# Attention beside a fused expert layer: scores one tile ahead, the product with v cut at block boundaries, the sums of v earlier, and tasks that come at 0.8 and 0.7

## The chip, the cores and the metric

The kernel runs on one core of one Trainium2 chip. The metric is the time of one execution in microseconds (us) of device time; a time given for a kernel is the median of several executions. A profile shows one execution, with its own time.

## What is computed

There are three stages, all in float32. The first is attention over 8 batches, 8 heads, 576 queries and 64 channels, in which keys and values are first averaged over groups of 8 rows, so that each query meets 72 keys:

```python
k_p = k.reshape(B, H, Sp, pool, D).mean(axis=3)
v_p = v.reshape(B, H, Sp, pool, D).mean(axis=3)
scores = scale * np.matmul(q, k_p.transpose(0, 1, 3, 2))
scores = scores - np.max(scores, axis=-1, keepdims=True)
attn = np.exp(scores)
attn = attn / (np.sum(attn, axis=-1, keepdims=True) + 1e-09)
return np.matmul(attn, v_p).astype(np.float32)
```

Its output, as 4608 tokens of 512 channels, goes through `((x @ w1) * (x @ w2)) @ w3 @ w_out` and that through `relu(x @ w_in)**2 @ w_out2`. The wide products are made of three float32r products each (high and low parts of both operands).

## The kernel before

The kernel is laid out around TensorE (PE). A first stretch (`fold`) multiplies `w3 @ w_out` into one matrix W. Then come nine **blocks** of 512 tokens. A block has eight **units**: in a unit `stage_ab` runs 24 matmuls of x with w1 and w2 (`ps_w`, 512 columns each), VectorE (DVE) and ScalarE (ACT) multiply the two results and split them into `gt`, and two units later `stage_w` runs 12 matmuls with W (`acc`). After the ninth block the third stage fills the rest of the span; the change does not touch its code.

Attention is no stage of its own. `build_tasks` writes its work out as a list of small **tasks**, and `attend` takes tasks from that list at each tick. A tick comes after every 6 matmuls of a block. Each tick adds `rate[0]` to a credit; once the credit reaches `visit[0]`, tasks run while a credit of 1 is left. A task may name what must be done first (`need`); if that is missing the list stops there and the credit is capped at 3. At the start of a block `until(tokens_ready(...))` ticks on with no matmul of a block between, until all tokens of the block are there.

A batch has five tiles of queries (128 rows, the last 64), in two halves: tiles 0 and 1 (256 queries), and tiles 2 to 4 (320). For a tile g the tasks are: `pe_s` (two halves: scores `ps_s`, then maxima `mx` on DVE, eight exponentials into `att` on ACT, and on GpSimd, called POOL here, the division by the sums), `place_rem` (POOL copies the keys past the 128th into `rem`), and `pe_t` (part 0 transposes `att` into `ps_t`, part 1 transposes `rem`; ACT and DVE split the results into `aT` and `aR`). At the end of a half `pe_av` runs once for each of the four pairs of heads: four matmuls into `ps_av` with `vl` and `vr` (the pooled v, split), then ACT copies the high part and DVE subtracts the low part into the block's operand `x` (chunk `x_blk_c` of block blk). A half that lies across a block boundary needs the later block's buffers, so its tasks wait until the block two before that is through (`("ab", last - 2)`).

All of `ps_s`, `ps_t`, `ps_av` and `ps_kt` (the turned keys) share two PSUM buffers, the pool `ps_at`. A task whose buffer is not free yet holds up PE, which runs its instructions in order; ACT and DVE too run theirs in the order written.

v of a batch is loaded in five pieces and summed on DVE (`vp` four times, and `ends`, L325), then `cut` and `cut_odd` split the sums into `vl` and `vr`. There is one buffer of each. k goes the same way through `kp` and `ends` (L329), and both share one queue, `back["kv"]`, of which one part is done per tick. From the second block on, the same ticks also feed the **quarters**: pieces of w_in and w_out2 that are prepared on ACT and DVE (`rq`, `raw`, `wq`, `sq`, `oq`) for the third stage.

Of the kernel before, what the change touches and what calls it, by code (L numbers as in the profile page):

```python
# [16 lines left out]
TB = 512  # L17
# [18 lines left out]
def attn_moe_moe2_kernel(  # L36
# [17 lines left out]
    B, H, S, D = q.shape  # L54
# [6 lines left out]
    NP = H // 2  # L61
# [8 lines left out]
    QT = []  # L70
    s0 = 0
# [3 lines left out]
    HALF = [[0, 1], [2, 3, 4]]  # L75
# [24 lines left out]
    done = set()  # L100
# [256 lines left out]
    def load_v(b):  # L357


        def parted(hi, lo, src, row):  # L360

            nc.scalar.activation(hi, src, ACTF.Copy, scale=row)
            nc.vector.scalar_tensor_tensor(
                lo, src, row, f32(hi), op0=ALU.mult, op1=ALU.subtract)

        def cut():
            for x in range(2):
                parted(vl[:, 0, :, x, :], vl[:, 1, :, x, :], vp, rows[:, x:x + 1])

        def cut_odd():  # L370
            vo = vr.rearrange("p (a b) t d -> p b a t d", a=2)[:, :, :, 1]
            for x in range(2):
                row = rows[:RB, 2 + x:3 + x]
                parted(vo[:RB, x], vo[2 * RB:, x], v5, row)
                nc.scalar.activation(vo[RB:2 * RB, x], v5, ACTF.Copy, scale=row)
            done.add(("v", b))

        return kv_parts(v, b, lambda j: vp[:, j, :], [cut, cut_odd])

    def pe_kt(b, part):  # L380

# [75 lines left out]
    def pe_s(g, half):  # L457
        b, i = divmod(g, len(QT))
        s0, n = QT[i]
        hf = 0 if i in HALF[0] else 1  # L460
        c0 = s0 - QT[HALF[hf][0]][0]
        flush("q", (b, hf))
        t = qts[b, hf]
        ps = ps_at.tile([P, TB], F32, tag="at", name="ps_s")
        hs = NP // 2
        for x in range(hs):
            hp = half * hs + x
            nc.tensor.matmul(  # L468
                ps[:n, x * 2 * SP:(x + 1) * 2 * SP], t[:, hp, c0:c0 + n],
                kbd[:, hp].rearrange("p a s -> p (a s)"), start=True, stop=True)  # L470
        sv = ps[:n, :NP * SP].rearrange("p (h s) -> p h s", s=SP)
        a = att[g % 3]
        h0 = half * NP
        av = a[:n, :H * SP].rearrange("p (h s) -> p h s", s=SP)
        mx = at_p.tile([P, NP], F32, tag="mx", name="mx", bufs=2)
        if half == 0:
            sums[g] = at_p.tile([P, H], F32, tag="sm", name="sm", bufs=2)
        sm = sums[g]

        scale = 1.0 / (POOL * D ** 0.5)  # L480

        nc.vector.reduce_max(mx[:n], sv, axis=AX.X)
        nc.vector.tensor_scalar(mx[:n], mx[:n], -scale, None, op0=ALU.mult)  # L483
        for h in range(NP):
            nc.scalar.activation(  # L485
                av[:, h0 + h], sv[:, h], ACTF.Exp, bias=mx[:n, h:h + 1], scale=scale,
                accum_out=sm[:n, h0 + h:h0 + h + 1])
        if half == 0:
            return

        nc.vector.tensor_scalar(sm[:n], sm[:n], 1e-9, float(POOL), op0=ALU.add, op1=ALU.mult)
        nc.vector.reciprocal(sm[:n], sm[:n])
        nc.gpsimd.tensor_mul(av, av, sm[:n].unsqueeze(2).to_broadcast([n, H, SP]))

        if g < 2 * len(QT) + 1:
            place_rem(g)

    def place_rem(g):
        n = QT[g % len(QT)][1]
        a = att[g % 3]  # L500
        rems[g] = at_p.tile([P, 2, RR], F32, tag="rem", name="rem")
        for x in range(2):
            nc.gpsimd.tensor_copy(
                rems[g][:n, x].rearrange("p (i c s) -> p i c s", i=3, c=2),
                a[:n, x * 4 * SP:(x + 1) * 4 * SP].rearrange("p (c w) -> p c w", c=2)[:, :, P:]
                .unsqueeze(1).to_broadcast([n, 3, 2, RM]))

    def pe_t(g, part):
# [18 lines left out]
        nc.scalar.copy(rem[:, :, c0:c0 + n], ps[:RR, :2, :n])  # L527
        dl = rem[RB:2 * RB, :, c0:c0 + n]
        nc.vector.tensor_sub(dl, ps[RB:2 * RB, :2, :n], f32(dl))
        if 2 * len(QT) <= g < NG - 1:  # L530
            place_rem(g + 1)

    def pe_av(b, hf, hp):
        hi, lo, rem = atts[b, hf]
        s0 = QT[HALF[hf][0]][0]
        w = sum(QT[i][1] for i in HALF[hf])
        ps = ps_at.tile([P, TB], F32, tag="at", name="ps_av")
        st = [vl[:, i, hp].rearrange("p a d -> p (a d)") for i in range(2)]
        for m in mm3(ps[:, :w], [(st, [t[:, hp, :w] for t in (hi, lo)])], last=False):
            m()  # L540
        nc.tensor.matmul(
            ps[:, :w], vr[:, hp].rearrange("p a d -> p (a d)"), rem[:, hp // 2, :w],
            start=False, stop=True)
        t0 = b * S + s0
        pieces = []
        o = 0
        while o < w:
            blk, c = divmod(t0 + o, TB)
            n = min(w - o, TB - c)
            pieces.append((blk, c, o, n))  # L550
            o += n

        for blk, c, o, n in pieces:
            nc.scalar.copy(xt_tile(blk, hp)[:, 0, c:c + n], ps[:, o:o + n])
        for blk, c, o, n in pieces:
            t = xt_tile(blk, hp)
            nc.vector.tensor_sub(t[:, 1, c:c + n], ps[:, o:o + n], f32(t[:, 0, c:c + n]))  # L557
        done.add(("av", b, hf, hp))

    NG = B * len(QT)  # L560

    def s_end(hf):
        return QT[HALF[hf][-1]][0] + QT[HALF[hf][-1]][1]

    def build_tasks(first_k, first_v):
# [49 lines left out]
        for g in range(NG):  # L615
            b, i = divmod(g, len(QT))
            hf = 0 if i in HALF[0] else 1

            if g < 2 * len(QT):
                if g + 1 != len(QT):  # L620
                    ahead_of(g)
            else:
                if g == 2 * len(QT):
                    ahead_of(g)
                if g + 1 < NG:
                    ahead_of(g + 1)
            if i == HALF[hf][0]:
                put_pend(len(pend))
            for part in range(2):
# [3 lines left out]
                for fn in first_v:  # L633
                    put(fn)
            if i == HALF[hf][-1]:
                need = [("v", b)]

                last = (b * S + s_end(hf) - 1) // TB
                if last >= 2:
                    need.append(("ab", last - 2))  # L640
                for hp in range(NP):
                    def av(b=b, hf=hf, hp=hp):
                        pe_av(b, hf, hp)
                        if hf == 1 and hp == NP - 1 and b + 1 < B:
                            load_v(b + 1)
                    pend.append((need, av))
                if b < EARLY:
                    put_pend(len(pend))
            if g + 1 == len(QT):
# [23 lines left out]

    def tokens_ready(n):

        b, s = divmod(n, S)
        halves = [(bb, h) for bb in range(b) for h in range(2)]
        if s:
            halves.append((b, 0))
            if s > QT[HALF[1][0]][0]:  # L680
                halves.append((b, 1))
        return all(("av", bb, h, hp) in done for bb, h in halves for hp in range(NP))


    wt = {}
# [646 lines left out]
    hold_v[0] = False  # L1332
    pumps.append(feed_w12)
    until(lambda: tokens_ready(TB))
    rate[0] = 0.7
    visit[0] = 2.0

    late = []
# [35 lines left out]
    for i in range(NB):  # L1374
# [18 lines left out]
            pend.append((i, u))  # L1393
        done.add(("ab", i))
        if i == 1:
            rate[0] = 0.6
        if i == 0:
            until(lambda: not fh1)
            sec_p.release()
# [105 lines left out]
```

## Time and profile before

| | us |
|---|---|
| median of 3 runs | 1530.74 (1528.7 to 1532.65) |
| the profiled execution, its own time | 1529.85 |
| its span, first to last instruction | 1528.0 |
| PE busy in the span | 1492.2 |
| DVE busy | 1000.3 |
| ACT busy | 798.4 |

The span is 1.85 us shorter than the execution's own time, and that execution was 0.89 us below the median. PE is the engine that is busy nearly throughout.

### The profile page before, as it was taken

The numbers are of one execution on the slowest core, as the hardware profiler recorded it, in microseconds if no ns is written. First come the engines' busy times: TensorE is split into PE (matmuls) and PEld (weight loads), VectorE is DVE, ScalarE is ACT, GpSimd is POOL, SyncE is SP. The second block draws the span as 40 slices with busy tenths as digits, with TensorE's granted clock in tenths as the row PEclk, the third lists the DMA queues.
The fourth block names the chain that finished last, engine by engine and source line by source line (L and its number), as shares of the span: only waits on it lengthen the run. The fifth ranks groups of instructions, "written<-read, shape, count | busy, mean of one in ns | idle before, by whom it ended". The sixth has DMA issues, their size and how long they took to land.

```text
span 1528.0 us, 21290 instructions
## 1 busy us (share of the span) xinstructions
PE 1492.2 (98%) x6752; PEld 1200.6 (79%) x6752; DVE 1000.3 (65%) x1798; ACT 798.4 (52%) x1953; POOL 81.2 (5%) x144
## 2 busy tenths in 40 slices
PE   6899999999999999999999999999999999999998
PEld 3457778877888888878888888888888888888887
DVE  7988686676767477658245477759675967576542
ACT  6866465454545355545235575456445744464431
POOL 1011110101010011100000000000000000000000
PEclk9999999999999999999999999999999999999999
DMA  9545666566666657557539777777777777788752
GB/s 288 197 139 138 165 196 161 168 178 174 187 199 174 193 127 242 149 169 227 173 113 307 222 195 247 208 209 229 235 207 208 232 207 207 208 268 282 209 163 89
DMA packets 292783, 301.34 MB, mean 197 GB/s; under 512 B 119360, under 2 KB 184896, under 8 KB 292672
## 3 DMA queue, kind: packets, MB, share of 16 engines
q1 hardware_dynamic: 287488, 290.54, 65.3%
q10 hardware_dynamic: 5184, 9.44, 1.8%
q8 instruction: 55, 0.90, 0.2%
q14 instruction: 56, 0.46, 0.1%
HBM read 243.27 MB, written 56.62 MB: 196 GB/s over the span
## 4 chain that ended last, share of the span: by engine, by line
PE 71%; DVE 4%; ACT 2%; DMA 1%; issue 1%; ACTq 0%; DVEq 0%
PE o L1219 18%; PE ps_w L193 17%; PE acc L193 9%; PE ps_c L1117 5%; PE ps_a L1117 5%; PE ps_d L1117 5%; PE ps_h L193 3%; PE o L193 3%; PE ps_b L1117 3%; PE ps_s L468 1%; PE ps_av L193 1%; PE ps_t L521 1%; DVE gt L121 1%; DMA rq<-in_moe_w_in_dram 0%; ACT x2o L120 0%
## 5 line engine op out<-in xcount | busy, mean ns | idle before, releaser
L1219 PE MATMUL o<-gt,un 128*128 128x512 f32 x1344 | 329.4, 390 | 0.4
L1219 PEld LDWEIGHTS o<-gt,un 128*128 128x128 f32 x1344 | 251.9, 188 | 54.6 <-DVE gt L121 2.1
L121 DVE TENSOR_TENSOR gt<-gs,gt 128x512 fp32r<-128x512 f32 x240 | 164.9, 689 | 179.8 <-ACT gt L120 178.4
L193 PE MATMUL ps_w<-x,wt 128*128 128x512 f32 x960 | 240.7, 397 | 1.9 <-DVE x L557 0.9
L120 ACT CAST gt<-gs 128x512 fp32r<-128x512 f32 x240 | 148.5, 620 | 154.8 <-PE o L1219 88.0
L193 PE MATMUL acc<-gt,Wt 128*128 128x512 f32 x864 | 219.6, 397 | 0.0
L193 PEld LDWEIGHTS ps_w<-x,wt 128*128 128x128 f32 x960 | 175.5, 188 | 41.2 <-DVE x L557 2.7
L193 PEld LDWEIGHTS acc<-gt,Wt 128*128 128x128 f32 x864 | 160.6, 189 | 32.8 <-issue 0.8
L193 PE MATMUL ps_w<-x,un 128*128 128x512 f32 x768 | 184.5, 392 | 0.0
L193 PEld LDWEIGHTS ps_w<-x,un 128*128 128x128 f32 x768 | 142.5, 188 | 29.1 <-issue 0.2
L485 ACT ACTIVATE att<-ps_s,mx 128x72 f32<-128x72 f32 (+1 forms) x320 | 97.9, 323 | 49.0 <-DVE mx L483 48.6
L1124 ACT ACTIVATE r<-r 128x512 f32<-128x512 f32 x96 | 60.7, 632 | 118.8 <-DVE r L1154 118.3
L844 DVE TENSOR_TENSOR gf<-asb,ps_w 128x512 f32<-128x512 f32 x72 | 49.3, 685 | 75.1 <-PE ps_w L193 68.8
L1117 PE MATMUL ps_a<-x2o,un 128*128 128x512 f32 x384 | 97.5, 389 | 0.0
L1117 PE MATMUL ps_d<-x2o,un 128*128 128x512 f32 x384 | 97.5, 389 | 0.0
L1117 PE MATMUL ps_c<-x2o,un 128*128 128x512 f32 x384 | 97.5, 389 | 0.0
L1125 ACT ACTIVATE gs<-r 128x512 f32<-128x512 f32 x144 | 89.9, 629 | 3.6 <-DMA x2r<-x2d 2.0
L120 ACT CAST gt<-gf 128x512 fp32r<-128x512 f32 x72 | 44.8, 622 | 82.5 <-DVE gf L844 82.2
L1193 DVE TENSOR_TENSOR gs<-gs 128x512 f32<-128x512 f32 x128 | 86.5, 684 | 0.0
L1117 PEld LDWEIGHTS ps_d<-x2o,un 128*128 128x128 f32 x384 | 72.1, 188 | 15.0
L1117 PEld LDWEIGHTS ps_a<-x2o,un 128*128 128x128 f32 x384 | 72.1, 188 | 14.9
L1117 PEld LDWEIGHTS ps_c<-x2o,un 128*128 128x128 f32 x384 | 72.1, 188 | 14.9
(114 smaller groups left out, 1975.2 us busy)
## 6 DMA issues: line engine op xcount, KB each, us to landing
un<-u_w SPq DMA_DIRECT2D x128, 256.0 KB, 3.4
un<-u_A SPq DMA_DIRECT2D x128, 256.0 KB, 3.0
un<-u_S SPq DMA_DIRECT2D x128, 256.0 KB, 3.0
un<-u_oS SPq DMA_DIRECT2D x128, 256.0 KB, 3.0
un<-u_oA SPq DMA_DIRECT2D x96, 256.0 KB, 3.0
raw<-in_moe_w_dram SPq DMA_DIRECT2D x32, 512.0 KB, 5.3
raw<-in_moe_w_out_dram SPq DMA_DIRECT2D x24, 512.0 KB, 4.6
kv<-in_k_dram SPq DMA_DIRECT2D x32, 256.0 KB, 3.3
```

The lines of the kernel that those rows point to most:

```text
L120: nc.scalar.copy(hi, src)
L121: return (eng or nc.vector).tensor_sub(lo, src, f32(hi))
L193: (lambda a=a, b=b, i=i: nc.tensor.matmul(ps, a, b, start=first and i == 0, stop=last and i == n - 1))
L468: nc.tensor.matmul(ps[:n, x * 2 * SP:(x + 1) * 2 * SP], t[:, hp, c0:c0 + n], kbd[:, hp].rearrange("p a s -> p (a s)"), start=True, stop=True)
L485: nc.scalar.activation(av[:, h0 + h], sv[:, h], ACTF.Exp, bias=mx[:n, h:h + 1], scale=scale, accum_out=sm[:n, h0 + h:h0 + h + 1])
L521: nc.tensor.transpose(ps[:, c, :n], att[g % 3][:n, c * 2 * SP:c * 2 * SP + P], ident[:n, :n])
L844: front["dve"] = nc.vector.tensor_mul(gf, asb, pss[1])
L1117: nc.tensor.matmul(ps, l, r, start=first and j == 0, stop=j == len(todo) - 1, skip_group_check=True)
L1124: nc.scalar.activation(t, src, ACTF.Relu)
L1125: nc.scalar.activation(take(name), t, ACTF.Square)
L1193: d = nc.vector.tensor_sub(src, a, src)
L1219: nc.tensor.matmul(ob[x][o], l, r, start=u == 0 and m != 5 and j == 0, stop=u == NU - 1 and j == 2, skip_group_check=True)
```

## The change

Four things change. (1) Scores run one tile ahead of the transposes throughout (before, from the third batch on, two tiles ahead), with three `att` buffers as before; the copy into `rem` is again made right behind the scores, and `place_rem` is gone. (2) A half that lies across a block boundary is multiplied with v in two pieces, cut at the boundary: six of the sixteen halves, with pieces of 192 and 128, 128 and 192, 64 and 256, 192 and 64, 128 and 128, and 64 and 192 columns. Each piece has a need of its own, and a task then does two pairs of heads. (3) The sums of v of the next batch are queued once v of this batch is split (before: after the last product with it); the split itself follows the last product, or the sums if these come later. (4) The pace is 0.8 a tick instead of 0.7 from the first block, and 0.7 instead of 0.6 from the third.

```diff
             done.add(("v", b))
-
-        return kv_parts(v, b, lambda j: vp[:, j, :], [cut, cut_odd])
+            if b + 1 < B:
+                load_v(b + 1)
+
+        def summed():
+            done.add(("vs", b))
+            if b in cut_now:
+                cut()
+                cut_odd()
+
+        cuts_v[b] = [cut, cut_odd]
+        return kv_parts(
+            v, b, lambda j: vp[:, j, :], [cut, cut_odd] if b == 0 else [summed])
+
+    cuts_v = {}
+    cut_now = set()
+
+    def read_v(b):
+
+        if b + 1 == B:
+            return
+        cut_now.add(b + 1)
+        if ("vs", b + 1) in done:
+            for fn in cuts_v[b + 1]:
+                fn()
...
-        if 2 * len(QT) <= g < NG - 1:
-            place_rem(g + 1)
-
-    def pe_av(b, hf, hp):
+
+    def av_pieces(b, hf):
+
+        t0 = b * S + QT[HALF[hf][0]][0]
+        w = HWS[hf]
+        cut = TB - t0 % TB
+        if cut >= w or (t0 + cut) // TB < 2:
+            return [(0, w)]
+        return [(0, cut), (cut, w - cut)]
+
+    def pe_av(b, hf, hp, q0, w):
...
-            if g < 2 * len(QT):
-                if g + 1 != len(QT):
-                    ahead_of(g)
-            else:
-                if g == 2 * len(QT):
-                    ahead_of(g)
-                if g + 1 < NG:
-                    ahead_of(g + 1)
+            if g + 1 != len(QT):
+                ahead_of(g)
...
+                pieces = av_pieces(b, hf)
+                for q0, w in pieces:
+                    need = [("v", b)]
+                    last = (b * S + s_end(hf) - HWS[hf] + q0 + w - 1) // TB
+                    if last >= 2:
+                        need.append(("ab", last - 2))
+                    for hp in range(0, NP, len(pieces)):
+                        def av(b=b, hf=hf, hp=hp, q0=q0, w=w, n=len(pieces)):
+                            for x in range(hp, hp + n):
+                                pe_av(b, hf, x, q0, w)
+                            if hf == 1 and hp + n == NP and q0 + w == HWS[hf]:
+                                read_v(b)
+                        pend.append((need, av))
...
-    rate[0] = 0.7
+    rate[0] = 0.8
...
-            rate[0] = 0.6
+            rate[0] = 0.7
```

What this does to the order of instructions shows at the start of the third block (block 2). On PE, before, behind 12 matmuls with W (`acc`) of the last block, the products of batch 2's second half (320 columns, all four pairs of heads) stand apart, with other matmuls between them:

```order
L193 MATMUL ps_av_2845<-aT0_2415,vl_101 128x320
L193 MATMUL ps_av_2845<-aT1_2416,vl_101 128x320
L193 MATMUL ps_av_2845<-aT0_2415,vl_101 128x320
L541 MATMUL ps_av_2845<-aR_2417,vr_102 128x320
L193 MATMUL acc0_2254<-gt_2712,Wt_995 128x512 x2
L468 MATMUL ps_s_2855<-kbd_103,qT1_2476 128x144 x2
L193 MATMUL ps_w1_2907<-x_2_0_1896,wt_431 128x512 x3
```

On PE with the change, behind 12 matmuls with W and 6 of x with w1, the second piece of that half (192 columns) stands there with all four pairs of heads in one run. These are its last row of the second pair, the third and the fourth pair, and what follows:

```order
L563 MATMUL ps_av_2884<-aR_2371,vr_102 128x192
L193 MATMUL ps_av_2892<-aT0_2369,vl_101 128x192
L193 MATMUL ps_av_2892<-aT1_2370,vl_101 128x192
L193 MATMUL ps_av_2892<-aT0_2369,vl_101 128x192
L563 MATMUL ps_av_2892<-aR_2371,vr_102 128x192
L193 MATMUL ps_av_2900<-aT0_2369,vl_101 128x192
L193 MATMUL ps_av_2900<-aT1_2370,vl_101 128x192
L193 MATMUL ps_av_2900<-aT0_2369,vl_101 128x192
L563 MATMUL ps_av_2900<-aR_2371,vr_102 128x192
L537 MATMUL ps_t_2921<-ident_96,att0_104 128x128 x4
L193 MATMUL ps_w1_2868<-x_2_2_1984,wt_769 128x512 x3
```

The first piece (128 columns) has moved ahead into the block before, and 16 matmuls of the second, with a transpose behind them, stand in one piece. The same shape, four pairs in a run, stands at the starts of blocks 1, 6 and 7; at those of blocks 3 and 5 there are two runs of two pairs, with 4 matmuls and 1 matmul between.

On DVE at the same place, before, behind the product `gf` of the last unit, one sum of k is left, and the first low part of `x` is sixth:

```order
L329 TENSOR_REDUCE ends_98<-kv_2745 64x64
L482 TENSOR_REDUCE mx_2803<-ps_s_2800 128x4
L121 TENSOR_TENSOR gt_2816<-gf_2815,gt_2816 128x512
L483 TENSOR_SCALAR mx_2803<-mx_2803 128x4
L446 STREAM_TRANSPOSE qT0_2755<-qraw_2763 128x256
L557 TENSOR_TENSOR x_2_0_1896<-ps_av_2845,x_2_0_1896 128x128
L557 TENSOR_TENSOR x_3_0_2851<-ps_av_2845,x_3_0_2851 128x192
```

On DVE with the change, behind the same `gf`, four sums of k stand ahead of the first `x`, and the split of v for the next batch follows inside the run:

```order
L329 TENSOR_REDUCE kp_97<-kv_2585 128x64
L950 TENSOR_TENSOR oq_3116<-sq_3018,oq_3116 128x512
L121 TENSOR_TENSOR gt_2843<-gf_2842,gt_2843 128x512
L329 TENSOR_REDUCE kp_97<-kv_2836 128x64
L329 TENSOR_REDUCE kp_97<-kv_2854 128x64
L329 TENSOR_REDUCE ends_98<-kv_2863 64x64
L579 TENSOR_TENSOR x_3_0_2881<-ps_av_2876,x_3_0_2881 128x192
L579 TENSOR_TENSOR x_3_1_2889<-ps_av_2884,x_3_1_2889 128x192
L950 TENSOR_TENSOR oq_3177<-sq_3018,oq_3177 128x512
L579 TENSOR_TENSOR x_3_2_2897<-ps_av_2892,x_3_2_2897 128x192
L363 SCALAR_TENSOR_TENSOR vr_102<-ends_98,rows_100,vr_102 32x2x64
L363 SCALAR_TENSOR_TENSOR vl_101<-vp_99,rows_100,vl_101 128x4x64 x2
```

Four sums of k instead of one now stand between `gf` and the first `x`. At the start of block 1 four sums of k stand there too, two of them ahead of each of two groups of `x`.

On DVE in unit 3 of block 2, before, the last sum of v and the split of batch 3 stand directly ahead of the `x` of the first products with it:

```order
L325 TENSOR_REDUCE ends_98<-kv_3165 32x128
L482 TENSOR_REDUCE mx_3221<-ps_s_3218 64x4
L914 TENSOR_TENSOR sq_3299<-sq_3299,wq_3068 128x256
L363 SCALAR_TENSOR_TENSOR vr_102<-ends_98,rows_100,vr_102 32x2x64
L483 TENSOR_SCALAR mx_3221<-mx_3221 64x4
L844 TENSOR_TENSOR gf_3253<-asb_3196,ps_w2_3198 128x512
```

With the change these sums of batch 3 stand in units 2 to 4 of block 1, and its split at the start of block 2, as the rows above show.

## Rows read from the trace of the kernel before

**Rows 1.** Windows: length, busy us of each engine, granted clock, DMA share, GB/s.
```profile
120.00:710.00 590.00, 580.08 (x2801) 472.47 (x2800) 399.58 (x821) 309.60 (x1020) 66.25 (x114) 0.99 0.62 177
140.00:175.00 35.00, 32.25 (x150) 24.53 (x148) 30.82 (x61) 21.10 (x76) 6.10 (x9) 0.95 0.71 194
315.00:335.00 20.00, 17.82 (x83) 14.36 (x83) 15.60 (x31) 10.23 (x27) 1.99 (x3) 0.91 0.56 160
710.00:1528.00 818.00, 813.02 (x3583) 671.61 (x3582) 500.37 (x777) 402.28 (x691) 0.00 (x0) 1.00 0.71 211
```

**Rows 2.** Waits of PE from 120 to 710 us: total us, times, longest.
```profile
PE ps_av L541 <- DVE vr L363: 2.2, 1, 2.2
PE ps_t L521 <- issue: 2.0, 1, 2.0
PE ps_s L468 <- ACT att L485: 1.1, 2, 0.9
PE ps_av L193 <- DVE vl L363: 0.9, 2, 0.6
PE ps_w L193 <- DVE x L557: 0.9, 2, 0.5
PE ps_av L193 <- ACT vl L362: 0.6, 1, 0.6
PE ps_av L193 <- DVE x L557: 0.5, 2, 0.3
```

**Rows 3.** Timeline, 317 to 321 us: start, us, engine, instruction [idle before <-releaser].
```profile
317.21 1.09 PE L193 MATMUL acc<-gt,Wt 128*128 128x512 f32 x4
...
320.49 0.36 PE L541 MATMUL ps_av<-aR,vr 96*128 96x256 f32 x1 [2.18 <-DVE vr L363]
```

**Rows 4.** Timeline, 145 to 148 us: maxima of two halves, then a transpose.
```profile
145.40 0.24 DVE L483 TENSOR_SCALAR mx<-mx 128x4 f32<-128x4 f32 x2
...
147.08 1.02 PE L521 MATMUL ps_t<-ident,att 128*128 128x128 f32 x4 [2.03 <-issue]
```

**Rows 5.** Timeline of PE: spacing of matmuls of 256, 512 and 64 columns.
```profile
237.90 0.51 PE L193 MATMUL ps_av<-aT,vl 128*128 128x256 f32 x3
...
238.85 1.55 PE L193 MATMUL acc<-gt,Wt 128*128 128x512 f32 x6
240.24 2.89 PE L193 MATMUL ps_w<-x,un 128*128 128x512 f32 x12
...
266.40 0.46 PE L521 MATMUL ps_t<-ident,att 64*128 64x64 f32 x4
266.79 1.43 PE L193 MATMUL acc<-gt,Wt 128*128 128x512 f32 x5
```

**Rows 6.** Timeline, 152 to 154 us: a product's way out of PSUM.
```profile
152.26 0.28 PE L541 MATMUL ps_av<-aR,vr 96*128 96x256 f32 x1
...
152.58 0.37 ACT L554 CAST x<-ps_av 128x256 fp32r<-128x256 f32 x1 [1.27 <-PE ps_av L541]
...
153.35 0.42 DVE L557 TENSOR_TENSOR x<-ps_av,x 128x256 fp32r<-128x256 f32 x1
...
153.82 0.42 PEld L193 LDWEIGHTS ps_av<-aT,vl 128*128 128x128 f32 x3 [0.29 <-DVE x L557]
```

**Rows 7.** Groups by line and form: busy us, mean ns of one | idle before.
```profile
L329 DVE TENSOR_REDUCE vp<-kv 128x64 f32<-128x512 f32 x32 | 33.4, 1065 | 1.5 <-DMA kv<-in_v_dram 1.4
L557 DVE TENSOR_TENSOR x<-ps_av,x 128x192 fp32r<-128x192 f32 x16 | 5.6, 349 | 4.3 <-ACT x L554 4.3
L554 ACT CAST x<-ps_av 128x192 fp32r<-128x192 f32 x16 | 5.1, 322 | 8.5 <-PE ps_av L541 8.4
```

**Rows 8.** Timeline, start of block 3: a sum of k ahead of `x`.
```profile
365.13 0.49 ACT L554 CAST x<-ps_av 128x64 fp32r<-128x64 f32 x2 [2.64 <-PE ps_av L541]
...
365.88 1.03 DVE L329 TENSOR_REDUCE kp<-kv 128x64 f32<-128x512 f32 x1
...
367.10 0.73 PE L193 MATMUL ps_w<-x,wt 128*128 128x512 f32 x2 [0.51 <-DVE x L557]
```

More of the change, by code (lines that the diff above doesn't have):

```diff
@@ L493, in pe_s @@
         nc.gpsimd.tensor_mul(av, av, sm[:n].unsqueeze(2).to_broadcast([n, H, SP]))
[L495 to L500, printed above, removed]
         rems[g] = at_p.tile([P, 2, RR], F32, tag="rem", name="rem")
@@ L529, in pe_t @@
         nc.vector.tensor_sub(dl, ps[RB:2 * RB, :2, :n], f32(dl))
-        if 2 * len(QT) <= g < NG - 1:
-            place_rem(g + 1)
-    def pe_av(b, hf, hp):
+    def av_pieces(b, hf):
[6 more added lines that the diff above has]
+    def pe_av(b, hf, hp, q0, w):
         hi, lo, rem = atts[b, hf]
-        s0 = QT[HALF[hf][0]][0]
-        w = sum(QT[i][1] for i in HALF[hf])
+        s0 = QT[HALF[hf][0]][0] + q0
         ps = ps_at.tile([P, TB], F32, tag="at", name="ps_av")
         st = [vl[:, i, hp].rearrange("p a d -> p (a d)") for i in range(2)]
-        for m in mm3(ps[:, :w], [(st, [t[:, hp, :w] for t in (hi, lo)])], last=False):
+        for m in mm3(ps[:, :w], [(st, [t[:, hp, q0:q0 + w] for t in (hi, lo)])], last=False):
             m()
         nc.tensor.matmul(
-            ps[:, :w], vr[:, hp].rearrange("p a d -> p (a d)"), rem[:, hp // 2, :w],
+            ps[:, :w], vr[:, hp].rearrange("p a d -> p (a d)"), rem[:, hp // 2, q0:q0 + w],
             start=False, stop=True)
@@ L557, in pe_av @@
             nc.vector.tensor_sub(t[:, 1, c:c + n], ps[:, o:o + n], f32(t[:, 0, c:c + n]))
-        done.add(("av", b, hf, hp))
+        done.add(("av", b, hf, hp, q0))
     NG = B * len(QT)
@@ L635, in build_tasks @@
             if i == HALF[hf][-1]:
[L636 to L646, printed above, removed]
+                pieces = av_pieces(b, hf)
[11 more added lines that the diff above has]
+                        pend.append((need, av))
                 if b < EARLY:
@@ L674, in tokens_ready @@
     def tokens_ready(n):
[L676 to L682, printed above, removed]
+        for b in range(B):
+            for hf in range(2):
+                t0 = b * S + QT[HALF[hf][0]][0]
+                for q0, w in av_pieces(b, hf):
+                    if t0 + q0 < n and any(
+                            ("av", b, hf, hp, q0) not in done for hp in range(NP)):
+                        return False
+        return True
     wt = {}
```

## The prediction

> **What bounds the kernel now.** I read the windows first, stretch by stretch. Behind 710 us PE is busy for 813.0 of 818 us at the full granted clock [rows 1]. The third stage and the last blocks lie there, which the change leaves alone, so nothing is to be won there. From 120 to 710 us, where attention runs between the matmuls of the blocks, PE is busy for 580.1 of 590 us, so 9.9 us are idle, and the mean granted clock is 0.99 [rows 1]. Two windows say where the clock fell: 0.95 over 35 us and 0.91 over 20 us. That is 35 x 0.05 + 20 x 0.09 = 3.6 us of PE time at either place together, about 1.8 us each. So all that this change can win by filling PE is near 9.9 + 3.6 = 13.5 us, plus what each wait costs beyond the gap that is shown. I work that out once: four matmuls from 317.21 us would have been through by 317.21 + 4 x 0.23 = 318.13, the next one starts at 320.49, which is 2.36 us lost where the view shows a gap of 2.18 [rows 3]. So 0.2 us go on top of every wait.
>
> The list of PE's waits in that stretch tells what they were for [rows 2]. Three things stand out. v was late: 2.2 + 0.9 + 0.6 = 3.7 us in four waits for `vr` and `vl`. The low parts of `x`, or the exponentials that hold a PSUM buffer, were late at places where several products stand close together: 0.9 + 0.5 + 1.1 = 2.5 us in six waits. And 2.0 us went into one transpose.
>
> **The change part by part.** *Earlier sums of v.* The split of v then waits for its last reader alone, and stands a whole half ahead of the first product with it. All four waits should go: 3.7 + 4 x 0.2 = 4.5 us. The longest of them, 2.18 us, was followed by the second of the two drops of the clock [rows 3, 1], so that one's 1.8 us goes too: -6.3 us. The sums themselves (four of 1.07 us for a batch, and one longer [rows 7]) move to other places on DVE, which is busy for 400 of the 590 us [rows 1]. Bounds: 0, if another operand is late at the same places, and -6.3.
>
> *The product in two pieces.* What belongs to the earlier block is multiplied ahead of time, so the first matmuls of a block no longer wait for `x` that was just made. The six waits of the second kind should go: 2.5 + 6 x 0.2 = -3.7 us, bounds 0 and -3.7.
>
> It adds matmuls: six halves x 4 pairs x 4 = 96 more, with the same columns in all. Eight matmuls of 256 columns take 0.95 us (237.90 to 238.85), 119 ns each; six of 512 take 1.39 us, 232 ns [rows 5]. A line through these has a fixed part of some 6 ns, so the least is 96 x 6 ns = 0.6 us. The other end is the shortest matmul in these rows, 64 columns at 0.39/4 = 98 ns with a change of work in it. If no piece is quicker than that, pieces of 64, 128 and 192 columns cost 64, 36 and 7 ns more than the line: 48 x 64 + 64 x 36 + 64 x 7 ns = 5.8, with the fixed part 6.4 us. I take 2.0 us, nearer the line, because those transposes stand four in a row between two changes of work.
>
> [...] No row here has a product of 128 columns by itself.
>
> *The new runs of products.* What is late next? Only two PSUM buffers serve all of attention, and a product leaves its buffer by an ACT copy and then a DVE subtraction. From the last matmul of a product (152.26) to the load for the next one in that buffer (153.82) went 1.56 us, of which DVE was late by 0.40 (ACT was through at 152.95, DVE began at 153.35) [rows 6]. So 1.2 us with both free, for 256 columns; for 192 columns ACT takes 0.32 instead of 0.37 and DVE 0.35 instead of 0.42 [rows 7], hence 1.1. In a run of four pairs a product of 192 columns takes 4 x 91 ns = 0.36 us. The first gives its buffer back at 0.27 + 1.1 = 1.37 us, the third could have begun at 0.72, so PE waits for 0.65 us; what follows the fourth waits again for the third's buffer, another 0.65. That is 1.3 us a run, four runs: +5.2. At block 5 (pieces of 64 columns, one matmul between) the same reckoning gives 0.4 twice: +0.8. At four more places a half of scores stands right behind two pairs, or two matmuls later, at 0.3 each: +1.2.
>
> At the starts of blocks 1 and 2 DVE is late as well, because four sums of k come ahead of `x`. At block 2, from the last matmul of the old block: `gf` 0.7, three `kp` and an `ends` near 1.07 each [rows 7], `oq` and `gt` 0.7 each, 6.4 us until the first `x`. PE is at the third pair after 18 x 0.23 + 0.72 = 4.9 us, so it waits until 6.4 + 0.35, for 1.9 us rather than 0.65. At block 1 it is 0.7 + 4 x 1.07 + 0.7 + two `x` at 0.35 + a transposed q near 0.4 = 6.8 us against 5.4, also 1.1 more than 0.65. Together +2.3. The trace has such a place already: at the start of block 3 ACT was through with `x` at 365.62, DVE stood in a sum of k until 366.91, and PE waited for that `x` [rows 8]. The runs come to 5.2 + 0.8 + 1.2 + 2.3 = 9.5 us. Bounds: 3 us, if half of the runs find other delays that cover them, and 13, if ACT and DVE are busy with quarters wherever the runs stand.
>
> *One tile ahead.* Between the second half of a tile's scores and its transpose there are still the scores of the next tile and the transposes of the one before, except for the last tile. I cost it at nothing; that matmuls of the blocks lie between covers it. Where the cover is gone it looks like the transpose at 147.08: it waited for a buffer that scores held because their maxima came late from DVE (145.40) [rows 4]. That stretch is one where DVE is busy for 30.8 of 35 us [rows 1], and the tasks stand there one tile ahead before and after. I leave its 2.0 us and its 1.8 us of clock in place; bounds -3.8 and +4, the latter if the sums of v for batch 2, which now fall into it, push it further (4 x 1.07 us and a longer one).
>
> *The pace* moves no work by itself; it spreads tasks, and its worth is in the terms above. Some preparation of quarters slips behind the ninth block, where DVE has 318 of 818 us free and ACT 416 [rows 1]: nothing, at most +3.
>
> **The sum.** -6.3 - 3.7 + 2.0 + 9.5 = +1.5 us against the profiled execution's own 1529.85, so 1531.4 us; the median of the runs is 0.9 us above that execution, so 1532.3, and I say 1532. What is won at v and at the old bunches is paid for by new ones, within what a measurement of this kernel can tell from no change (0.3%, 4.6 us).
>
> **The rivals.** *Faster: the runs cost little.* ACT and DVE empty a product while PE is held up by something else anyway, and the term of 9.5 falls to 1 to 2 us. Then -6.3 - 3.7 + 2 + 1.5 = -6.5, 1524 us. For it: before, runs of two pairs stood in the trace without a wait between them [rows 5]. Against it: two buffers suffice for two pairs and not for four. Chance 0.28.
>
> *Slower: a run stalls so long that the clock falls.* Both drops in the stretch came with a single idle gap of 2.0 us or more (2.03 and 2.18) [rows 4, 3]. The waits at blocks 1 and 2 are forecast at 1.8 and 1.9 us, just short of that. From 2.0 us on each would cost 1.8 us of clock, and waits of that length mean that ACT and DVE lag, so the runs are at 12 to 13: -10 + 2 + 12.5 + 3.6 = +8, 1539 us. Chance 0.17. [...] The trace bears out only long gaps here: in 335 to 710 us it has several waits and no drop.
>
> *Slower: the DVE-bound stretch at 140 to 175 us grows* by up to 4 us, as worked out above: 1536 us. Chance 0.10.
>
> **How the numbers follow.** The forecast, with its own range of 1527 to 1536, has the remaining 0.45. Faster by over 0.3% is the first rival, 0.28; slower by over 0.3% the other two, 0.27. The range takes in the nearer part of the fast rival and of the slow one: 1524 to 1539.
>
> **What the profile will show.** Right: no wait of PE for `vr` or `vl` from 120 to 710 us, and no drop of the clock near 320 us. Right for the runs: waits for `x` (of `ps_av`, and of `ps_t` or `ps_s` behind them) at the starts of blocks 1, 2, 6 and 7, near 1.3 us at 6 and 7 and 2 to 2.5 at 1 and 2. Right for the extra matmuls: 128-column products near 66 ns apart. The transpose near 145 us still waits. Idle PE time from 120 to 710 us would then be near 12 us instead of 9.9. Wrong, if the runs show no waits (fast), or if there are drops of the clock at starts of blocks (slow).

## The result, and the profile after

The changed kernel takes 1549.37 us (median of 4 runs, 1547.2 to 1550.88) where the kernel before takes 1530.83 in the same runs: 1.0121 times as long, 95% interval 1.0102 to 1.0139. The forecast was 1532 with a range of 1524 to 1539, so the time lies 10 us above the range. The profiled execution has a span of 1547.0 us, 19.0 more than before.

The windows of the changed kernel come first (columns as in [rows 1]). The first three rows cut the span where the work is the same as at 120 and 710 us before; the other four are the places where the clock fell.

```profile
0.00:118.00 118.00, 96.47 (x374) 55.31 (x375) 100.34 (x202) 86.98 (x248) 14.97 (x30) 1.00 0.66 209
118.00:728.00 610.00, 590.41 (x2895) 485.26 (x2894) 397.55 (x810) 307.96 (x1009) 67.87 (x114) 0.99 0.60 170
728.00:1547.00 819.00, 813.81 (x3583) 671.43 (x3581) 505.14 (x788) 405.25 (x698) 0.00 (x0) 1.00 0.71 211
136.00:146.00 10.00, 6.27 (x25) 4.88 (x24) 8.47 (x18) 6.56 (x24) 0.01 (x1) 0.84 0.59 155
190.00:208.00 18.00, 17.21 (x86) 14.47 (x85) 12.07 (x27) 7.55 (x32) 0.64 (x2) 0.91 0.65 206
281.00:299.00 18.00, 14.02 (x60) 11.66 (x59) 11.29 (x21) 6.79 (x16) 1.10 (x4) 0.81 0.85 266
606.00:624.00 18.00, 15.59 (x72) 12.65 (x72) 10.61 (x23) 8.84 (x18) 0.47 (x2) 0.91 0.88 275
```

The whole loss lies where attention runs: 610 us against 590 [rows 1], while what follows takes 819 against 818 and what precedes it 118 against 120 (there the kernel before lost 3.4 us to a drop of the clock near 31 us, and the changed kernel's profile has none). PE is idle for 19.6 us of the stretch instead of 9.9. The clock fell at four places instead of two, and the windows price them: 10 x 0.16 + 18 x 0.09 + 18 x 0.19 + 18 x 0.09 = 8.3 us, where before it was 3.6. The drop near 320 us is gone; those at the starts of blocks 1, 2 and 6 (190, 281 and 606 us) are new.

What PE waited for in that stretch (total us, times, longest), to be held against [rows 2]:

```profile
PE ps_av L193 <- DVE x L579: 7.8, 6, 3.9
PE ps_t L537 <- issue: 4.7, 3, 3.7
PE ps_s L490 <- DVE x L579: 4.6, 5, 2.1
PE ps_t L537 <- DVE x L579: 0.9, 3, 0.4
PE ps_t L542 <- issue: 0.6, 1, 0.6
PE ps_w L193 <- ACT wt L1325: 0.4, 1, 0.4
PE ps_av L193 <- DVE aR L545: 0.3, 1, 0.3
```

No wait for `vr` or `vl` is left, as forecast. In their place 13.3 us in 14 waits are for the low part of `x`, that is, for the way of a product out of its PSUM buffer. The four runs of four products have 7.9 us of them (0.8 at block 1, 3.9 at 2, 2.4 at 6, 0.8 at 7), and scores (`ps_s`) that stand behind other products have 4.4 in four waits.

The longest one, in the timeline of the start of block 2:

```profile
284.88 1.05 DVE L329 TENSOR_REDUCE kp<-kv 128x64 f32<-128x512 f32 x1 [0.16 <-DMA kv<-in_k_dram]
...
285.37 0.50 PE L193 MATMUL ps_av<-aT,vl 128*128 128x192 f32 x3
285.57 0.77 ACT L576 CAST x<-ps_av 128x192 fp32r<-128x192 f32 x2 [2.40 <-PE ps_av L563]
...
285.71 0.27 PE L563 MATMUL ps_av<-aR,vr 96*128 96x192 f32 x1
...
287.42 1.01 DVE L329 TENSOR_REDUCE kp<-kv 128x64 f32<-128x512 f32 x1 [1.49 <-DMA kv<-in_k_dram]
288.46 1.01 DVE L329 TENSOR_REDUCE ends<-kv 64x64 f32<-64x512 f32 x1
...
289.51 0.62 DVE L579 TENSOR_TENSOR x<-ps_av,x 128x192 fp32r<-128x192 f32 x2
...
289.92 0.96 PE L193 MATMUL ps_av<-aT,vl 128*128 128x192 f32 x3 [3.94 <-DVE x L579]
```

ACT had copied both products by 286.34. DVE should have subtracted from 285.93 on, but the next instruction in its order was a sum of k whose load had not landed; it stood for 1.49 us, did that sum and the one behind it, and came to `x` at 289.51. The third product of the run waited for 3.94 us. At the start of block 6 it is ACT that stands (the run begins with the first two lines):

```profile
612.62 0.44 PE L193 MATMUL ps_av<-aT,vl 128*128 128x128 f32 x3
...
612.90 0.27 PE L563 MATMUL ps_av<-aR,vr 96*128 96x128 f32 x1
...
613.35 0.27 PE L563 MATMUL ps_av<-aR,vr 96*128 96x128 f32 x1
...
614.38 0.65 ACT L151 ACTIVATE raw<-raw 128x512 f32<-128x512 f32 x1 [1.03 <-DMA raw<-in_moe_w_out_dram]
614.94 0.25 ACT L576 CAST x<-ps_av 128x128 fp32r<-128x128 f32 x1
...
615.57 0.55 PE L193 MATMUL ps_av<-aT,vl 128*128 128x128 f32 x3 [1.95 <-DVE x L579]
```

The copy stands behind the unpacking of a weight of the third stage, which waits for its own load. Not every holder waits for a transfer: the scores at 485.88 us waited for 2.12 us because DVE worked through four other instructions ahead of `x` (483.63 to 485.57), none of which waited.

The new matmuls show in PE's timeline: products of 64, 128 and 192 columns, and one of 320.

```profile
529.93 0.50 PE L193 MATMUL ps_av<-aT,vl 128*128 128x64 f32 x3
...
530.26 0.28 PE L563 MATMUL ps_av<-aR,vr 96*128 96x64 f32 x1
```

```profile
613.01 0.50 PE L193 MATMUL ps_av<-aT,vl 128*128 128x128 f32 x3
```

```profile
453.61 0.60 PE L193 MATMUL ps_av<-aT,vl 128*128 128x320 f32 x3
454.05 0.31 PE L563 MATMUL ps_av<-aR,vr 96*128 96x320 f32 x1
```

From the first to the fourth matmul of a product go 0.33 us at 64 columns (529.93 to 530.26), 0.34 at 128 (613.01 to 613.35), 0.34 at 192 (285.37 to 285.71) and 0.44 at 320 (453.61 to 454.05). So 64, 128 and 192 columns all cost about 112 ns, 256 cost 119 [rows 5] and 320 cost 147. Half the columns don't cost half the time. One distance is shorter: the first product at block 6 takes 0.28 us (612.62 to 612.90) where the next takes 0.34.

### The profile page after: what moved, and what is told of

Same layout as the page of the kernel before. It is cut to its first block, busy times and chain, and to the rows that moved or that the text cites. A ratio compares the mean times of both kernels' runs of the same rounds, so it can differ in the third digit from the quotient of the medians.

```text
span 1547.0 us, 21451 instructions
## 1 busy us (share of the span) xinstructions
PE 1500.7 (97%) x6848; PEld 1212.0 (78%) x6848; DVE 1003.0 (65%) x1798; ACT 800.2 (52%) x1953; POOL 82.8 (5%) x144
## 4 chain that ended last, share of the span: by engine, by line
PE 72%; DMA 3%; DVE 3%; ACT 2%; issue 1%; SPq 1%; ACTq 0%; DVEq 0%
PE ps_w L193 18%; PE o L1238 18%; PE acc L193 9%; PE ps_a L1136 5%; PE ps_c L1136 5%; PE ps_d L1136 5%; PE ps_h L193 3%; PE o L193 3%; PE ps_b L1136 2%; DMA raw<-in_moe_w_out_dram 2%; PE ps_s L490 2%; PE ps_av L193 1%; PE ps_t L537 1%; DVE gt L121 1%; SPq L473 0%
## 5 line engine op out<-in xcount | busy, mean ns | idle before, releaser
L193 PE MATMUL ps_w<-x,wt 128*128 128x512 f32 x960 | 246.6, 404 | 0.5 <-ACT wt L1325 0.4
L193 PE MATMUL acc<-gt,Wt 128*128 128x512 f32 x864 | 214.8, 393 | 0.0
L193 PEld LDWEIGHTS ps_w<-x,wt 128*128 128x128 f32 x960 | 179.1, 192 | 37.1 <-issue 1.0
L859 ACT COPY asb<-ps_w 128x512 f32<-128x512 f32 x72 | 42.5, 590 | 78.1 <-PE ps_w L193 78.1
```

Of the source, the lines that this page charges most:

```text
L193: (lambda a=a, b=b, i=i: nc.tensor.matmul(ps, a, b, start=first and i == 0, stop=last and i == n - 1))
L859: nc.scalar.copy(asb, ps)
```

## The experiments

Each kernel was timed beside the kernel before on the same chip; its medians there are 1529.6 to 1530.8 us, so a difference between two lines is good to about 1 us. For each kernel the table splits the blocks' time, from the start of unit 1 of block 0 to the ninth block's last matmul with w1 or w2. It is made from the starts of PE's matmuls: each matmul's distance to the next start, less the plain distance for its shape (227 ns for 512 columns, 122 for 144, 109 for transposes of 128, half of that taken for 64, and the values above for products). The plain distances add up to 661.0 us, and to 669.9 in every kernel that has the 96 narrow matmuls. "Clock" is half the length of the clock's drops: the granted clock in a drop is 0.50, as from 290 to 296 us of the changed kernel, where matmuls of 512 columns start 427 ns apart. "Waits" is all that is left, with the small cost of each change of work. "Starts" is what of clock and waits falls between the last matmul with w1 or w2 of a block and the end of the next one's first unit, for blocks 1 to 7. The split is of one profiled execution of each kernel (that of the 7th lay 2.6 us above its median), and a drop more or less can be the execution's: the mean granted clock is 0.995 to 1.000 in 47 executions of the kernel before, and 0.993 or 0.994 in all four of the changed kernel.

| kernel | us | ratio, 95% | blocks | narrow | clock | waits | starts |
|---|---|---|---|---|---|---|---|
| before | 1529.9 | | 696.8 | 0 | 3.4 | 32.4 | 10.4 |
| after | 1549.4 | 1.0121 (1.0102 to 1.0139) | 717.4 | 8.9 | 8.5 | 39.1 | 19.1 |
| 1: v alone | 1525.96 | 0.9971 (0.9961 to 0.9980) | 695.1 | 0 | 1.7 | 32.5 | 8.8 |
| 2: whole products | 1527.38 | 0.9984 (0.9974 to 0.9995) | 695.1 | 0 | 1.7 | 32.4 | 7.8 |
| 3: pairs apart | 1535.09 | 1.0031 (1.0019 to 1.0043) | 703.6 | 8.9 | 3.4 | 30.3 | 1.9 |
| 4: old pace | 1544.5 | 1.0095 (1.0081 to 1.0109) | 711.0 | 8.9 | 3.4 | 37.7 | 14.0 |
| 5: 96 matmuls alone | 1546.09 | 1.0112 (1.0097 to 1.0128) | 713.1 | 8.9 | 8.5 | 34.7 | 20.5 |
| 6: k's sums held | 1551.75 | 1.0146 (1.0132 to 1.0159) | 717.7 | 8.9 | 8.5 | 39.4 | 16.6 |
| 7: v, one ahead | 1527.54 | 0.9985 (0.9976 to 0.9994) | 698.0 | 0 | 1.7 | 35.3 | 8.2 |
| 8: v, new pace | 1525.14 | 0.9976 (0.9964 to 0.9987) | 693.7 | 0 | 1.7 | 31.1 | 4.9 |
| 9: no preparation | | | 708.5 | 8.9 | 6.8 | 31.9 | 13.5 |
| 10: 9, whole products | | | 691.1 | 0 | 3.4 | 26.7 | 4.6 |
| 11: all held | 1620.08 | 1.0607 (1.0584 to 1.0631) | 712.5 | 8.9 | 6.8 | 35.8 | 9.8 |

The 9th and 10th put work off to a later place, so only their blocks are read, not their whole time (1657 and 1644 us, one execution each).

**1, v alone.** The kernel before with the sums of v moved and nothing else:

```diff
+            if b + 1 < B:
+                load_v(b + 1)
...
-                        if hf == 1 and hp == NP - 1 and b + 1 < B:
-                            load_v(b + 1)
+                        if hf == 1 and hp == NP - 1:
+                            read_v(b)
```

> The kernel before with the earlier sums of v alone (whole products, two tiles ahead in the later batches, 0.7 and 0.6). Theory, runs of products cost the time: no run of four products is here, v is no longer late at 2.2 + 0.9 + 0.6 us, and the drop of the clock near 320 us goes, so 4 to 6 us below before, 1525 us. Rival, v's earlier sums crowd VectorE and the DMA queues and so make x late: 5 to 15 us above before, 1536 to 1545. Rival, the pace of tasks is to blame: as the theory, 1525.

Measured 1525.96, 4 us below before, the number of the first theory. In its windows from 140 and from 300 us the clock near 320 us is full now, and DVE in the crowded stretch is as busy as before (31.06 against 30.82 us, [rows 1]):

```profile
140.00:175.00 35.00, 30.77 (x141) 22.85 (x140) 31.06 (x62) 20.45 (x75) 5.03 (x8) 0.95 0.66 179
300.00:335.00 35.00, 33.85 (x164) 27.26 (x163) 24.07 (x47) 16.76 (x51) 3.02 (x3) 1.00 0.67 185
```

No wait for `vr` or `vl` is left, but others stand elsewhere (118 to 725 us):

```profile
PE ps_t L543 <- issue: 3.1, 1, 3.1
PE ps_s L490 <- DVE aT L121: 2.0, 2, 1.8
```

The waits in the table are therefore as long as before (32.5 and 32.4), and within the blocks only 1.7 us of clock are won. Another 2 us of the profile's gain lie ahead of the blocks, where the drop of the clock near 31 us was 3.4 us long instead of 6.8; its length differs from profile to profile (0, 3.4 or 6.8). So the gain of 4 us is shown, its source only in part. The earlier sums are no part of the loss; they are the part of the change that pays.

**2, whole products.** The changed kernel without the cut.

```diff
-        if cut >= w or (t0 + cut) // TB < 2:
+        if True:
             return [(0, w)]
```

> The changed kernel with whole products (no product is cut at a block boundary), all else as changed. Theory, runs of products cost the time: the runs of four at the starts of blocks 1, 2, 6 and 7 are gone, and the halves of scores behind two narrow pairs too; the starts fall from some 22 us over the pure work to about 10, so 12 to 17 us below the changed kernel, 1532 to 1537. Rival, the pace: the tasks still come at 0.8 and 0.7, so at most 4 us below it, 1545 to 1549. Rival, v's sums: also 1545 to 1549.

Measured 1527.38: 22 us below the changed kernel, more than the 12 to 17 expected. The cut is the whole loss; without it, pace and sums of v cost nothing against before.

**3, pairs apart.** The cut stays; one pair in a task instead of two.

```diff
-                    for hp in range(0, NP, len(pieces)):
-                        def av(b=b, hf=hf, hp=hp, q0=q0, w=w, n=len(pieces)):
+                    for hp in range(0, NP, 1):
+                        def av(b=b, hf=hf, hp=hp, q0=q0, w=w, n=1):
```

> The changed kernel, products still cut at block boundaries, but one pair of heads in a task where it had two, so that at most two products stand next to each other with six or more block matmuls behind them. The work is the same. Theory, runs of four: 8 to 12 us below the changed kernel, 1537 to 1541 (the 1.3 to 2 us of 96 more matmuls and the DVE-bound stretch near 140 us stay). Rival, the cut itself (more matmuls, more evacuations on ScalarE and VectorE): no change, 1547 to 1550. Rival, the pace or v's sums: no change either, or a little slower because there are more tasks.

Measured 1535.09: 14.3 us below the changed kernel, with the same matmuls, evacuations and pace. This is the price of two pairs in one task, and so of four products in a run. The starts fall from 19.1 to 1.9 us. What is left against whole products, 7.7 us, is near the 8.9 of the narrow matmuls; in the split, 1.7 us more of clock and 2.1 less of waits go with them.

**4, old pace.** 0.7 and 0.6 instead of 0.8 and 0.7.

> The changed kernel with the old pace of tasks, 0.7 and 0.6. Theory, runs of four: runs of four still stand at the starts of blocks 1 and 6 and in block 7, behind other work than before; 3 to 6 us below the changed kernel, 1543 to 1546. Rival, the pace crowds VectorE and the DMA queues: 12 us or more below it, 1531 to 1537. Rival, v's sums: no change, 1546 to 1550.

Measured 1544.5, as the theory of the runs had it: three long runs are left, six products at the start of block 1 and four at blocks 6 and 7, and the loss shrinks by 5 us without going.

**5, the 96 matmuls alone.** Whole products, but each product of the six halves is written as two groups of four matmuls into the two parts of one PSUM buffer.

```diff
+        c = TB - t0 % TB
+        for o, n in [(0, w)] if c >= w or (t0 + c) // TB < 2 else [(0, c), (c, w - c)]:
+            for m in mm3(ps[:, o:o + n], [(st, [t[:, hp, o:o + n] for t in (hi, lo)])], last=False):
+                m()
```

> The kernel of the second experiment (whole products, 1527.4 us) with the matmuls of the six halves cut in two column pieces that go to the same PSUM buffer: 96 more matmuls with the same columns in all, no more tasks, evacuations or buffers. Theory, a product's matmul takes 110 us/1000 or more however few its columns are (in the changed kernel those of 64, 128 and 192 columns start 112, 112 and 113 ns apart, of 256 119, of 320 147): 8.9 us for the 96, so 1536. Rival, the line of the prediction (2.0 us): 1529.5. Rival, its upper bound (6.4 us): 1534.

Measured 1546.09, 18.7 us above the second experiment, where 8.9 was expected. The miss is one of design. With other matmuls the order of PE came out otherwise too, and groups of four stand in runs: eight at the start of block 1, six at that of block 2, four at blocks 5, 6 and 7. The table splits it: 8.9 us of spacing as computed, 6.8 more of clock, 2.3 more of waits. The windows of its starts of blocks 1 and 2:

```profile
190.00:208.00 18.00, 16.09 (x81) 13.73 (x80) 12.44 (x27) 6.86 (x25) 0.64 (x2) 0.81 0.61 184
281.00:299.00 18.00, 15.27 (x73) 12.85 (x72) 11.68 (x26) 7.47 (x27) 2.66 (x5) 0.81 0.64 187
```

The clock fell for 6.8 us at either place, and the waits there were no longer than 1.5 us. So this run does not price the spacing by itself; the distances of the matmuls do.

**6, k's sums held.** The changed kernel; in the first unit of a block no load or sum of k or v of a later batch is issued.

```diff
+        elif begun[0] == 1:
+            pass
         elif back["kv"] and not wait_kv[0] and (not held[0] or len(back["kv"]) > 9):
...
+            begun[0] = int(i > 0 and u == 0)
             stage_ab(i, u)
```

> The changed kernel, but while the first unit of a block is written, no load and no sum of k or v of a later batch is issued; they come a unit later. Theory, VectorE stands in sums of k (one of them waiting for its DMA) while the x that would free a PSUM buffer is behind them, and the long wait drops the clock: at the start of block 2 the wait of 3.9 us falls to about 1, and the drop of 6.8 us there goes (3.4 us), so 1542 to 1544. Rival, two buffers alone make the wait in a run of four: at most 1 us is won, 1548 to 1550. Rival, the sums come late somewhere else instead: 1549 or above, with waits for kp or vl.

Measured 1551.75, no gain. The start of block 2 shows why:

```profile
287.22 0.58 PE L193 MATMUL ps_av<-aT,vl 128*128 128x192 f32 x3 [0.84 <-DVE x L582]
287.63 0.28 PE L566 MATMUL ps_av<-aR,vr 96*128 96x192 f32 x1
289.72 0.62 ACT L949 CAST oq<-sq 128x512 fp32r<-128x512 f32 x1 [3.44 <-DMA u_A<-oq]
290.25 0.53 ACT L579 CAST x<-ps_av 128x192 fp32r<-128x192 f32 x2
...
291.39 0.96 PE L193 MATMUL ps_av<-aT,vl 128*128 128x192 f32 x3 [3.48 <-DVE x L582]
```

The wait for the first buffer fell from 3.94 to 0.84 us, as the theory had it. But the next one is 3.48: now ACT stood in `oq`, a conversion of a quarter whose buffer is freed when a store to HBM is through, with both copies of `x` behind it. Taking one holder away let the next one hold.

**7 and 8, one tile ahead, and the pace.** The second experiment with the old pace, and the first with the new one.

> The second experiment with the old pace, 0.7 and 0.6: the earlier sums of v and scores one tile ahead, with whole products. It splits the 1.4 us between the first experiment (v alone, 1526.0) and the second (1527.4). If the pace costs it: 1526. If one tile ahead costs it (transposes that wait for exponentials just made): 1527.5.

> The first experiment (the earlier sums of v alone, 1526.0 us) with the new pace, 0.8 and 0.7. If the pace costs the 1.4 us between the first and the second experiment: 1527.5. If one tile ahead costs them: 1526. A result below 1525 would be a pace that helps this order.

Measured 1527.54 and 1525.14. The pace costs nothing: 0.2 us between the 7th and the 2nd, 0.8 between the 8th and the 1st, inside the intervals. That holds for whole products; with the cut, the new pace stands 4.9 us above the old one (4th experiment; the intervals just overlap). One tile ahead costs about 2 us: 1.6 between the 7th and the 1st, 2.2 between the 2nd and the 8th; the intervals of either pair overlap, so only the agreement of the two speaks for it. The 1st and the 8th are faster than the kernel before by some 0.3%; between the two the intervals don't decide.

**9 and 10, no preparation.** The changed kernel and the second experiment, with the preparation of quarters put off until attention's tasks are all issued. PE's order stays the same but for a few matmuls. The sums of k move too, because their queue waits on the quarters (`held`): at block 2 they are through by 268 us and stand ahead of no `x` there.

```diff
-        if ring and quarters and not operands and ticks[0] % rate_q[0] == 0:
+        if ring and quarters and not tasks and not operands and ticks[0] % rate_q[0] == 0:
```

> The changed kernel with the preparation of quarters put off until attention has no task left. The blocks and the products stand as in the changed kernel, with the same runs of four at the starts of blocks 1, 2, 6 and 7; only the end of the program gets longer, so this run is read up to the end of the ninth block alone. Theory, x leaves late because ScalarE and VectorE work on, and wait for, preparation that stands ahead of it: the excess over plain spacing in the blocks falls from 47.6 us to about 35, the longest wait at a start to under 1 us, and the drops of the clock at the starts of blocks 1, 2 and 6 go. Rival, two PSUM buffers alone do it: the starts keep most of their 19 us, with waits for x of 0.7 us and more in every run and the drops still there. Either way the spacing of the narrow matmuls (112 ns) stays, 8.9 us.

> The second experiment (whole products) with the preparation put off in the same way; read up to the end of the ninth block alone. It is the control of the ninth: theory (preparation delays x, and runs of four suffer most): the excess falls from 34.1 us to about 28, and what is left between this run and the ninth is the 8.9 us of matmuls and 3 to 6 us of waits for two buffers. Rival (two buffers alone): the distance to the ninth stays near the 21 us that lay between the second experiment and the changed kernel.

In the 9th the excess over plain spacing is 38.7 us (6.8 + 31.9), not 35, and two starts tell why. Preparation began at 594 us all the same, before the last products: `fetch` runs it too, when a unit that it needs is not stored. So block 2 ran without it and block 6 with it. Block 2:

```profile
286.40 0.77 ACT L576 CAST x<-ps_av 128x192 fp32r<-128x192 f32 x2 [3.10 <-PE ps_av L563]
...
286.75 0.80 DVE L579 TENSOR_TENSOR x<-ps_av,x 128x192 fp32r<-128x192 f32 x2 [2.73 <-ACT x L576]
287.16 0.58 PE L193 MATMUL ps_av<-aT,vl 128*128 128x192 f32 x3 [0.36 <-DVE x L579]
...
288.75 0.52 PE L537 MATMUL ps_t<-ident,att 128*128 128x128 f32 x3 [0.45 <-DVE x L579]
```

Block 6:

```profile
607.35 0.62 ACT L946 CAST oq<-sq 128x512 fp32r<-128x512 f32 x1 [2.73 <-DMA u_A<-oq]
607.87 0.26 ACT L576 CAST x<-ps_av 128x128 fp32r<-128x128 f32 x1
...
608.95 0.90 PE L193 MATMUL ps_av<-aT,vl 128*128 128x128 f32 x3 [4.14 <-DVE x L579]
```

The run of four at block 2, which waited for 3.94 us in the changed kernel, waits for 0.36 + 0.45 us with the two engines free; the run at block 6 waits for 4.14 with ACT standing in `oq`. Outside block 6 the waits for `x` come to 3.9 us in this run, and to 10.9 in the changed kernel. From the 9th to the 10th the blocks' time falls by 17.4 us: 8.9 for the narrow matmuls, 6.1 at the start of block 6 (7.8 against 1.7), and only 2.4 for all else. So two buffers alone cost little; what costs is a copy of `x` that stands behind preparation, above all behind an instruction that waits for a transfer.

**11, all held.** Both kinds of preparation held during the last unit of a block and the first of the next.

> The changed kernel with no step of preparation, of k's or of v's loads and sums issued while the last unit of a block and the first of the next are written; all of it comes later instead. Theory: fewer of the instructions that wait for a transfer stand ahead of x at the starts, so 4 to 8 us below the changed kernel, 1541 to 1545. Rival, the delayed work only stands ahead of the next x, as in the sixth experiment: 1548 to 1553.

Measured 1620.08, a miss. The blocks took 4.9 us less than in the changed kernel and the starts fell from 19.1 to 9.8, but quarters that were not ready in time stopped the third stage. Its waits from 835 us on:

```profile
PE o L1241 <- DMA un<-u_oA: 51.4, 5, 22.3
PE o L1241 <- ACT wq L152: 7.9, 1, 7.9
```

The preparation can't simply be put off.

## Why the prediction was wrong

The steps from kernel to kernel are: the sums of v -3.9 us (to the 1st experiment), one tile ahead and the pace +1.4 (to the 2nd), the cut with pairs apart +7.7 (to the 3rd; its 96 matmuls are 8.9 by their spacing), runs of four +14.3 (to the changed kernel). They add up to 19.5; the direct comparison, with runs of before of its own, gives 18.5. The prediction had -6.3, 0, -1.7 (2.0 for the added matmuls less 3.7 for the first waits) and 9.5 for them. So the two steps that failed most are the price of the cut itself, 9.4 us too low, and that of the runs, 4.8 too low; the clock is a part of the second.

*Earlier sums of v, forecast -6.3.* Right in direction: all four waits and the drop of the clock near 320 us are gone. The size is 4 us. The 4.5 us put down to the four waits did not come, because other waits of 1.2 to 3.1 us took their place in the first experiment.

*The added matmuls, forecast 2.0 within 0.6 to 6.4.* The step that failed is the line through 256 and 512 columns. Below 256 columns the distance doesn't fall: 112 ns at 64, 128 and 192, where the forecast had 66 for 128. A half of 320 columns cut into 128 and 192 costs 112 + 112 - 147 = 77 ns more for each of its 16 matmuls, cut into 64 and 256 it costs 112 + 119 - 147 = 84, and a half of 256 costs 112 + 112 - 119 = 105. With two, one and three of these, 16 x (2 x 77 + 84 + 3 x 105) = 8.8 us (8.9 in the table, from unrounded distances). The upper bound took 98 ns from four transposes with a change of work behind them, also too low, and it priced something else: most transposes of 64 columns start 61 to 64 ns apart. PE's weight loads show the same pace, 113 ns from load to load (612.95 to 613.29 for three); by single starts at the full clock the third load of a product comes 108 to 111 ns after the second at 64, 128 and 192 columns alike. Where the second load begins together with the first matmul (2 or 3 ns behind it), as it does in most products behind matmuls of 512 columns, the distance from the first matmul to the second falls to 30, 58 and 87 ns (three, six and five products; hence the 0.28 us above). So the matmuls can follow each other faster, and it is the pace of the loads that keeps them apart, as far as distances show it; no run changes the loads alone:

```profile
612.95 0.41 PEld L193 LDWEIGHTS ps_av<-aT,vl 128*128 128x128 f32 x3
613.29 0.19 PEld L563 LDWEIGHTS ps_av<-aR,vr 96*128 96x128 f32 x1
```

The profile's record of one load is 190 ns long (the last line), and these records overlap; the 113 ns are the distance of their starts.

*The first waits of a block, forecast -3.7.* They do go if the pieces stand apart: the starts take 7.8 us with whole products and 1.9 in the 3rd experiment. But most of it comes back elsewhere there, for one in a wait of 2.55 us for exponentials at 585 us, with a drop of the clock behind it; all in all the 3rd experiment lies only 1.2 us below what the 8.9 of the matmuls alone would give. In the changed kernel the runs put 19.1 at the starts.

*The new runs, forecast 9.5 within 3 to 13.* The place and the waiting instructions were right; the price is 14.3, of which 8.8 are waits (39.1 less 30.3) and 5.1 clock. For the four runs the forecast had 7.5 us (5.2 + 2.3) and 7.9 were measured, but that is luck: blocks 1 and 7 took less than forecast (0.8 each), blocks 2 and 6 more (3.9 and 2.4), and the four sums of k at block 1 held the first `x` up by under 0.4 us. The scores behind other products took 4.4, where the forecast had 1.2 for four places, and the clock took 5.1 instead of nothing. The step that failed is "1.2 us with both free". Where both were free, the sum was right or high: 0.36 + 0.45 us, against 0.65 twice. But in the changed kernel, at blocks 2 and 6, ACT or DVE stood in an instruction that waited for a transfer (1.49 us for a load of k, 1.03 for a weight), and every `x` stood behind it (the first begins at 289.51 and 614.94 us). The prediction counted the sums of k by their 1.07 us and not by the wait for their load; at block 2 that made 3.94 instead of 1.9.

*The clock.* The slow rival, with a chance of 0.17, is what happened at blocks 2 and 6, and more: the clock costs 5.1 us more than before (8.5 less 3.4). Its threshold of one idle gap of 2.0 us was wrong both ways. At 485.88 us a gap of 2.12 kept the full clock. At block 6 the gap was 1.95, and at block 1 the clock fell behind waits of 0.56 and 0.23 us in a run of 16 matmuls of 128 columns, as PE's timeline there shows:

```profile
199.06 0.55 PE L193 MATMUL ps_av<-aT,vl 128*128 128x128 f32 x3 [0.56 <-DVE x L579]
...
200.40 0.91 PE L490 MATMUL ps_s<-kbd,qT 128*128 128x144 f32 x4 [0.23 <-DVE x L579]
```

At block 7 a run of 16 matmuls of 192 columns, with waits of 0.35 and 0.45, kept the full clock. So did the run at block 1 itself in the 6th and 9th experiments, with the same waits (0.56 and 0.23 or 0.24). Their windows there:

```profile
191.00:209.00 18.00, 16.75 (x91) 14.00 (x90) 13.00 (x28) 8.22 (x32) 0.64 (x2) 1.00 0.63 208
193.00:211.00 18.00, 16.75 (x90) 13.96 (x89) 13.03 (x29) 8.35 (x33) 0.64 (x2) 1.00 0.63 207
```

So neither the run nor its waits decide by themselves. What does stays open.

*The DVE-bound stretch, forecast unchanged, at most +4.* Its transpose waits for 3.7 us instead of 2.03, but it stands 12 matmuls earlier. In all, clock and waits take 3.3 us more in block 0 than before (11.9 against 8.6, reckoned as in the table). They do so with whole products too (11.9), so this is not the cut's. With the earlier sums of v alone they take 10.2 and the wait is 3.1, so the sums of v seem to bear a part of it, as the upper bound of the prediction allowed for.

*One tile ahead, forecast nothing:* about 2 us. *The pace, forecast nothing:* right with whole products.

## What to carry to other kernels

Before a matmul is cut in pieces, look in a trace for the shortest distance between matmuls of the same type that each have weights of their own; here it was 112 ns at 192 columns and below, so a piece of a half of 256 cost nearly as much as the whole (119 ns), and a line through wide shapes misled. Where products leave PSUM through engines that also prepare later work, price their way out by what can stand ahead of them in those engines' order, transfers included, not by its own duration; and keep products apart by more other matmuls than such a stand lasts. Try the parts of a change one by one: here one of four won 4 us and another lost 22.

## What was not expected of the hardware

The matmuls of products of 64, 128 and 192 columns start 112 ns apart, all alike. The clock of TensorE fell for 3.4 us, near 200 us, behind waits of no more than 0.56 us, and in the 5th experiment twice for 6.8 us behind waits of no more than 1.5 us, each time in a run of narrow matmuls; the same run near 200 us, with the same waits, kept the full clock in two other experiments. In the kernel before it had fallen only behind gaps of 2.0 us and more in that stretch.
